# An attention and mixer kernel: 254 steps near its start in another order, other PSUM banks behind them, and 22 unread matmuls split in two

## The chip, the cores and the metric

The kernel runs on one core of a Trainium2 chip. The metric is the device time of one execution in microseconds (us), as the median of several runs. A difference of less than about half a per cent is near what the runs of one kernel differ by among themselves.

## The reference

Inputs are `q`, `k`, `v` of shape 8 x 8 x 576 x 64 (batches, heads, positions, head width) and four weight matrices, all float32. First comes block-causal attention (blocks of 64 positions), then a mixer: one layer pair over the positions (tokens), one over the channels.

```python
scores = (q @ k.T) / 8          # masked to block_i >= block_j, softmax over j
x = softmax(scores) @ v         # -> 8 x 576 x 512 (heads side by side)
xt = x.transpose(0, 2, 1)
h = relu(xt @ w_tok1) @ w_tok2  # 576 -> 256 -> 576
u = x + h.transpose(0, 2, 1)
h2 = relu(u @ w_ch1) @ w_ch2    # 512 -> 1536 -> 512
out = u + h2
```

## The kernel before

The kernel is one long program without loops at run time. Python code lists 1591 small **steps** (a step is a few instructions on one engine), and a written-out string, `ORDER` (L100), says which of them are issued, 1518 in all, in which order and on which engine. A word of it such as `269Tcbda` is step 269, on TensorE (T; A is ScalarE, D VectorE, P GpSimd with the DMAs that it issues, S the DMA queue of SyncE), and the letters behind it are the PSUM banks that the step takes: one bank for each letter, a to d ("mm" in the profile) and e to h ("late"). `placed` (L75) reads the words. Each engine runs its own steps strictly in the order of the words and waits where an operand is not ready.

A bank is taken by a TensorE step, filled, read by VectorE or ScalarE, and given back by the last step that reads it. There are eight banks. When a step takes a bank, its first matmul into it must wait until the last reader of the bank's earlier content has ended, so the letter decides on whom the step waits.

The profile calls the engines PE (TensorE), PEld (its weight loads), DVE (VectorE), ACT (ScalarE), POOL (GpSimd) and SP (SyncE). The steps that matter below, with the line of their instructions:

- Unread matmuls (`raise_clock`, emission at L371 and L378): 11 of 512 columns, then single ones of 256 columns, steps 45 to 154, of which the order issues 37 (45 to 81). They multiply zeros while the first inputs arrive, and nothing reads them.
- Score sets (`score_set`, L568): the scores of four heads in 32-row strips of the array; for batch 1 these are 269, 276, 281 (heads 0 to 3) and 301, 308, 313 (heads 4 to 7), for batch 2 among others 445 and 470. From batch 1 on each takes four banks. Their exponentials run on ACT (L774; L587 in batch 0): 270 to 273 belong to 269, one for each head and bank.
- Transposes of q and k by VectorE (L442): 259, 260, 262 and 263 for batch 1's heads 4 to 7.
- Clears of a tail block of the exponentials (`tail`, L601), on DVE or POOL: 217 and 236 for batch 0's heads 4 to 7.
- Head outputs (`head_out`): exponentials times v on PE (L618; batch 0's in two parts of 3 and 7 matmuls, such as 222 and 223 for head 4, 226 and 227 for head 5, 241/242 and 245/246 for heads 6 and 7), then a reciprocal (L638) and a product (L644) on DVE, which gives the bank back. The last 64 positions go apart (`ends_out`): PE L671 (230 and 249 for batch 0's later heads, 298 and 330 for batch 1), DVE L693 and L699 (193 and 194).
- The token layers: `token_up` (PE L809 and L813, then a relu on ACT L795 or DVE L797; 337, 339, 341, 343 for batch 0, 502 to 505 for batch 1) and `first_uT` or `token_mix` (PE L904).
- The channel layers: `channel_up` for batch 0 (PE L1032), later `channel_up_half` (L1105) and `channel_up_fast` (L1232), `channel_down_fast` (L1366), and transposes of four 128-column matmuls each (`turn`, L1388).

Loads of weights and of later batches go through POOL's DMA queue in the order of the words; outputs go through SP's. POOL's own steps and the DMAs that it issues share one queue.

Of the kernel before, what the change touches and what calls it, by code (L numbers as in the profile page):

```python
# [27 lines left out]
class Plan:  # L28
# [73 lines left out]
    47Tb 48Tb 49Ta 50Ta 37P 51Ta 52Ta 53Ta 54Ta 55Ta 56Ta 35P 57Ta 7D 174Tst 175T 34P 195A 58Ta 59Ta 60Ta  # L102
    61Ta 196A 62Ta 38P 197D 63Ta 31D 64Ta 65Ta 66Ta 176A 199Tt 36P 177A 178D 67Ta 179D 68Ta 33D 69Ta 255P 70Ta 200A
    180Ts 27D 198P 71Ta 72Ta 40P 73Ta 181A 29D 182Tt 157P 74Ta 75Ta 76Ta 183A 77Ta 201Ts 43P 78Ta 79Ta 80Ta 253D
    202A 42P 214Tt 254D 188Tb 189T 41P 215A 184Tc 11D 233Ts 6D 190D 191D 258P 192Td 211Ta 234A 220Tt 216P 256D 39P
    185T 257D 221A 81Tb 218Ts 155P 212D 213D 207Tb 235D 208T 186D 219A 158P 187D 237Tt 193D 209D 156P 203Ta 210D
# [4 lines left out]
    305A 425D 354Td 355T 302A 313Tcbfh 279A 356D 306P 387Tg 353A 267P 426D 384Td 315A 388T 266P 316A 404Ta 385T 317A  # L111
    268P 408Tb 314A 381Te 386D 405A 416Tf 427P 409D 390Tc 389A 307P 391T 333D 430P 372Td 392A 308Tabhg 167P 373T
    311A 334D 382T 168P 310A 369Tc 309A 370T 169P 417A 375Tb 335D 434P 312A 378Ta 379T 383A 433P 366Th 374A 367T
    422D 371A 436P 400Td 423D 376T 380A 289Tc 377A 295Ta 290D 298Tf 368A 291D 330Tb 296D 401A 297D 292Tc 299D 286Tg
    331D 332D 438Tadeh 300D 287D 293D 288D 324Tb 440A 294D 357Tf 325D 439A 321Tc 326D 363Tg 428D 442A 364T 322D 441A
    323D 450Tbdah 431D 365A 318Tc 429D 454A 358T 453A 319D 327Te 432D 360Tg 451A 320D 361T 452A 328D 329D 482Tcabh
    362A 443D 359D 502Te 444P 483A 435P 393D 485A 604P 484A 504Td 503A 437P 170D 486A 470Tcbag 595P 505A 171D 601P
    473A 445Tfehd 471A 172D 514Ta 448A 508Tc 472A 173D 515A 512Th 506Tb 446A 509D 510Ta 474A 513D 397Tcf 447A 475P
    507D 449A 476P 394D 598P 477Tbghe 398A 403Td 395D 480A 479A 511D 481A 493Th 396D 520Ta 478A 490Tg 518Te 521A
    494D 407T 406D 519A 495D 597D 464Ta 596D 455Te 461Th 410D 458Tb 399T 465D 491D 456D 457D 462D 459D 466D 411T  # L120
    463D 600D 402D 496Ta 522Te 412D 516Th 413T 523A 497D 599D 419S 517A 460D 762P 492D 499Te 414D 759P 467Tb
    612Thgcd 498D 526D 415T 336D 615A 616A 614A 530Tca 613A 487Td 500D 468D 469D 531Tg 533A 501D 617P 527D 545Thb
    532A 418D 618P 536T 611P 548A 524Te 488D 489D 534Tg 537A 525D 610P 551T 528D 535A 624Tdecf 605D 608P 552A 538T
    606D 628A 607P 540T 529D 627A 539D 678Th 626A 609P 603D 625A 549Tc 602D 679A 619Tdfge 541D 550A 546Th 622A 760D
    553T 623A 763D 543T 620A 547D 676Tg 621A 761D 544A 644Tdehf 542D 926P 677A 554D 555T 647A 764D 560Tag 648A 556D
    561Tc 929P 563A 680Th 557D 765P 562A 684Tf 681D 645A 566T 558T 685D 646A 564Tc 567A 649D 559D 651Tdhef 650P 565A
    768P 638Ta 653A 635Tb 772P 639D 568T 652A 640D 570T 636D 654A 637D 686Ta 569D 655A 656Tbdhe 571D 641Tc 660A 687D
    629Tf 659A 573T 642D 630D 689S 643D 632Ta 658A 631D 682Te 572D 657A 788Tcfdh 633D 634D 574A 673Tb 683D 790A
    670Ta 674D 789A 664Tg 688S 675D 671D 579Tef 672D 791A 665D 792A 666D 769D 783Tbagc 580A 667Td 784A 661Th 668D
    581T 785A 669D 662D 786A 663D 767D 787A 776Tdhba 582D 842Tc 779A 766D 778A 575D 932P 840Tb 780A 941P 770D 777A  # L130
    583Ta 930D 773P 841A 576D 843A 781P 820Tdgeh 939P 577D 585T 771P 821A 578D 824A 775P 584D 694Tbc 850Td 774P 690D
    697A 587T 586D 822A 935P 691D 823A 782P 692D 698Th 851D 848Tg 588D 699A 700T 849D 695Td 701A 704T 696D 702T 589T
    705D 703D 693D 808Tabde 931D 707T 590D 810A 844Tg 812A 846Th 845D 809A 793Tb 591T 708A 847D 811A 794D 795D 813P
    815Tacde 592D 814P 805Tb 1024P 819A 802Tg 594S 806D 818A 799Th 807D 854S 803D 724Tfe 817A 800D 709Tdb 801D 816A
    727D 710Tc 712A 725Th 927D 711A 728Ta 855S 928D 726A 715T 804D 796Tc 729A 934D 730T 716A 713Th 933D 731A 734T
    420S 797D 798D 714A 732T 593S 735D 943Tcgdf 733D 719T 945A 736D 717T 946A 720D 831Ta 944A 834Tg 718D 737T 947A
    722T 835D 836D 738A 828Td 948P 832D 833D 950Tgchf 723A 829D 830D 837Ta 721D 953A 852Tb 838D 952A 839D 857D 825Td
    951A 853D 876Tea 1036P 954A 877Tc 858D 856S 879A 826D 861Tbh 827D 1035P 878A 862Tg 859D 864D 891Tfd 949P 863A
    880Tc 940P 706D 894A 882T 739D 881A 942P 865Tg 897T 937D 866A 938P 867T 936D 883A 884T 860D 1021P 868A 871T 885D
    1030P 869T 898A 886T 872D 1027P 987Tbcef 870D 874T 887D 1034P 990A 895Tg 988A 875D 889T 991A 1007Te 740D 989A  # L140
    896A 890D 955Tbchf 741D 892Ta 959A 899T 1026D 956A 901T 893D 958A 1009Tf 957A 1008D 902D 975Tbach 1010D 972Te
    978A 904T 900D 979A 960Tf 1025D 969Tc 905A 743Tgh 961D 976A 973D 1122P 974D 962D 977A 970D 971D 982Tefdb 980D
    744A 981D 1022D 966Ta 984A 963Tc 1023D 745T 985A 967D 888D 1119P 986A 964D 965D 983A 1037P 995Td 968D 873A 998Tc
    746D 1050Tabfe 1033P 996D 999D 992Tg 1000D 1054A 749T 993D 1053A 994D 997D 1052A 1028D 1038Tcdge 1051A 1029D
    1004Tb 1041A 1031D 1001Ta 1125P 1040A 747Tf 1032D 1039A 1002D 1003D 1128P 1005D 1006D 1082Tdcga 1135P 748D
    1017Tb 1084A 742D 751T 1083A 1018D 1086A 750D 1042A 1045Tcdba 1085A 752D 1043P 753T 1047A 1131P 1121D 757S 1049A
    1120D 1044P 1048A 1077Tdegf 754D 1064Ta 1080A 1124D 1061Tb 755T 1046A 1065D 1062D 1063D 1079A 1078A 1070Tbcge
    1081A 756D 1067Td 1074A 1123D 1058Tf 1073A 1104Th 1066D 1059D 1071A 1060D 1130D 1072A 1055Ta 1143Tfbeg 1105A
    1056D 1075P 1057D 1015Tc 1134P 1068D 1146A 1127D 1013Ta 1145A 1069D 1102Th 1129D 1147A 1076D 1144A 1014D 1093Td
    1103A 1090Tb 1016D 1136Taegf 1126D 1020S 1099Tc 1137A 1094D 1114Th 1091D 1092D 1140A 1100D 1087Ta 1101D 1139A  # L150
    903D 1096Tb 1088D 1112Tc 1138A 1089D 758S 1108Tf 1095D 1115A 1141P 1113D 1106Ta 1132P 1175Tdgeh 1097D 1142D
    1098D 1011Tc 1133P 1107D 1179A 1336Tb 1177A 1012D 1178A 1109D 1168Tachg 1176A 1110Te 1116S 1171A 910Tdf 1170A
    1111D 1337A 1169A 1334Tc 1117S 911D 906D 1148Tbahe 912T 907D 1150A 1019S 1172A 1151A 916T 1173P 913D 1152A 1174P
    1149A 908D 1118S 1180Tadgh 909D 1153Tb 1183A 914Te 1154D 1184A 1155D 1181A 917D 1194Tb 1182A 1335D 1159Tg 1191Th
    1195D 1185Ta 1196D 1197Td 1160D 1192D 1165Tb 1193D 920T 915D 1161D 1198D 1199D 1166D 1188Th 1167D 921D 1162Td
    1156Tb 1189D 1249Tcg 1190D 918T 1163D 1164D 1252A 1200D 1201D 922T 1186D 919D 1157D 1255T 1158D 924S 1279Ted
    1187D 923D 1280Tb 1282A 1350Ta 1256A 1281A 1234Tch 1351A 1344Tf 1237A 1283Tb 1345D 1285T 1284A 1240T 1286A
    1338Ta 1241A 1250Tf 1339D 1253Te 1251A 1287T 1202D 1254A 1348Tc 1288D 1203D 1259T 1349A 1257T 1238Ta 1258D 1289T
    1239A 1235Tb 1290D 1342Tc 1236A 1244T 1291D 1343D 1356Tf 1242T 1245D 1219Tbc 1243D 1360Te 1260D 1220Ta 1361A
    1357D 1262T 1222A 1292T 1364S 1263D 1221A 1340Te 1247T 1293D 1223Ta 1341D 1358Td 1224A 1246D 1204Tfg 1359D 1248A  # L160
    1205Te 1225T 1207D 1206A 1264Tdh 1226A 1229T 1479D 1267A 1265Te 1230D 1208Tb 1266A 1227T 1480D 1209D 1270T
    1268Te 1271A 1214T 1269D 1212T 1354Td 1215D 1274T 1228D 1232T 1275D 1217T 1272T 1481D 1218A 1210T 1482D 1233A
# [1404 lines left out]
```

## Time and profile before

| | |
|---|---|
| runs, us | 283.47, 284.16, 284.64 (median 284.16) |
| the profiled execution: time | 284.69 us |
| its span, first to last instruction | 282.9 us |
| PE busy | 97% of the span |
| DVE busy | 84% |
| ACT busy | 63% |
| POOL busy | 26% |
| granted TensorE clock, mean | 1.000 |

The span is what the views of the trace cover; some 1.8 us of the execution lie outside it. Times in the views count from the start of the span. The view of the waits lists how long an engine stood still and on whose account. The view of the stretches gives the busy time of each engine between two points in time. The timeline lists instructions with their start, their length, line, shape and number. PE's matmuls overlap one another in these records, so the distance from start to start says more than a length.

### The profile page before, as it was taken

To read this page: it belongs to the slowest core of one execution; us is meant where nothing else is said; L and a number is where in the kernel's file an instruction comes from. 1 tells how busy PE (TensorE), PEld (TensorE's weight loads), DVE (VectorE), ACT (ScalarE), POOL (GpSimd) and SP (SyncE) were. 2 spreads that over 40 slices of the span, in tenths; PEclk is the share of its full clock that TensorE was granted. 3 is DMA by queue.
4 is the path that set the end of the run, shared out by engine and by line. 5 is a ranking of instruction groups with operands and counts; after the bars stand their busy time and mean duration, and the time that the engine had idled before them with its cause. 6 is when DMAs were issued, how large, how long until landed. Compare 5 with 4: busy or idle time off the path is not lost.

```text
span 282.9 us, 9352 instructions
## 1 busy us (share of the span) xinstructions
PE 275.3 (97%) x3982; PEld 204.0 (72%) x3982; DVE 238.9 (84%) x515; ACT 179.2 (63%) x331; POOL 72.7 (26%) x126
## 2 busy tenths in 40 slices
PE   7899999999999999999999999999999999999994
PEld 3466556588776788986877658756789876568884
DVE  3688669999889998999998979859896997579984
ACT  3798788953998856897879866274533744652200
POOL 8895870511631351063232221000000000000000
PEclk9999999999999999999999999999999999999999
DMA  7999999954979492999598594100044502200157
GB/s 163 160 178 192 202 190 206 152 92 86 142 87 139 87 150 56 250 109 170 66 118 139 56 188 60 70 10 19 0 84 95 196 0 76 75 1 2 74 151 224
DMA packets 64890, 31.95 MB, mean 113 GB/s; under 512 B 53200, under 2 KB 55888, under 8 KB 64848
## 3 DMA queue, kind: packets, MB, share of 16 engines
q0 software_dynamic: 44896, 17.49, 53.6%
q1 hardware_dynamic: 19520, 13.21, 18.2%
q8 instruction: 31, 0.51, 0.7%
q10 hardware_dynamic: 432, 0.66, 0.7%
q14 instruction: 11, 0.09, 0.1%
HBM read 35.85 MB, written 9.44 MB: 160 GB/s over the span
## 4 chain that ended last, share of the span: by engine, by line
PE 87%; DMA 4%; ACT 3%; POOL 3%; DVE 1%; issue 1%; POOLq 0%; DVEq 0%
PE late L1366 23%; PE mm L1105 8%; PE mm L1232 7%; PE mm L1366 7%; PE late L1232 6%; PE mm L568 6%; PE late L1105 6%; DMA qk_sb<-in_k_dram 4%; PE mm L618 4%; PE mm L809 3%; PE mm L904 2%; PE late L904 2%; PE late L618 2%; PE mm L1032 2%; ACT e_sb L774 2%; PE late L809 2%
## 5 line engine op out<-in xcount | busy, mean ns | idle before, releaser
L774 ACT ACTIVATE e_sb<-mm 128x512 bf16<-128x512 f32 x82 | 46.6, 606 | 13.1 <-PE late L568 9.4
L774 ACT ACTIVATE e_sb<-late 128x512 bf16<-128x512 f32 x86 | 48.5, 609 | 9.0 <-PE late L568 8.2
L442 DVE STREAM_TRANSPOSE qk_sb<-qk_sb 128x288 int32<-128x288 int32 (+1 forms) x65 | 41.8, 694 | 4.9 <-DMA qk_sb<-in_q_dram 1.8
L468 POOL DMA_DIRECT2D vals<-in_v_dram x45 | 36.9, 832 | 4.5 <-PE mm L618 2.4
L1366 PEld LDWEIGHTS <-gT 128*128 128x128 bf16 x336 | 32.0, 98 | 5.6 <-issue 0.4
L1366 PEld LDWEIGHTS <-sums 128*128 128x128 bf16 x324 | 31.3, 98 | 5.3 <-issue 0.4
L568 PEld LDWEIGHTS <-qk_sb 32*64 32x64 bf16 (+1 forms) x1152 | 19.0, 103 | 14.8 <-issue 11.1
L568 PE MATMUL mm<-qk_sb 32*64 32x64 bf16 (+7 forms) x504 | 26.9, 277 | 0.1
L618 PEld LDWEIGHTS <-e_sb 128*128 128x128 bf16 x640 | 23.1, 97 | 5.3 <-issue 2.2
L568 PE MATMUL late<-qk_sb 32*64 32x64 bf16 (+7 forms) x504 | 26.2, 283 | 0.6 <-issue 0.3
L1366 PE MATMUL late<-wd_sb,gT 128*128 128x256 bf16 x168 | 20.7, 273 | 0.0
L1366 PE MATMUL late<-wd_sb,sums 128*128 128x256 bf16 x168 | 20.6, 273 | 0.0
L1105 PEld LDWEIGHTS <-ws_sb 128*128 128x128 bf16 x192 | 18.2, 98 | 3.1 <-issue 0.9
L618 PE MATMUL mm<-vals,e_sb 128*128 128x65 bf16 x450 | 19.8, 193 | 0.5 <-DMA vals<-in_v_dram 0.3
L644 DVE TENSOR_TENSOR x_sb<-mm,rinv 128x256 bf16<-128x256 f32 x45 | 18.7, 422 | 1.3
L1412 DVE TENSOR_TENSOR o_sb<-late,u_sb 128x512 f32<-128x512 f32 x22 | 15.0, 684 | 3.6 <-PE late L1366 3.6
L1232 PEld LDWEIGHTS <-ws_sb 128*128 128x128 bf16 x120 | 11.7, 98 | 8.6 <-issue 0.2
L1105 PEld LDWEIGHTS <-wc_sb 128*128 128x128 bf16 x144 | 15.3, 114 | 1.5 <-issue 0.4
L1366 PE MATMUL late<-wc_sb,gT 128*128 128x256 bf16 x132 | 16.2, 273 | 0.0
L596 POOL COPY vals<-e_sb 128x256 bf16<-128x256 bf16 (+1 forms) x11 | 4.3, 393 | 39.7 <-ACT e_sb L774 39.6
L400 ACT COPY mm<-late 128x512 f32<-128x512 f32 (+1 forms) x16 | 9.1, 570 | 8.1 <-PE late L1232 5.4
L795 ACT ACTIVATE gT<-mm 128x512 bf16<-128x512 f32 x21 | 12.6, 616 | 1.9 <-PE mm L1105 0.9
(198 smaller groups left out, 630.7 us busy)
## 6 DMA issues: line engine op xcount, KB each, us to landing
out_dram<-o_sb SPq DMA_DIRECT2D x19, 256.0 KB, 3.0
qk_sb<-in_k_dram POOLq DMA_DIRECT2D x14, 288.0 KB, 6.0
qk_sb<-in_q_dram POOLq DMA_DIRECT2D x14, 288.0 KB, 5.9
vals<-in_v_dram POOLq DMA_DIRECT2D x28, 128.0 KB, 4.5
out_dram<-o_sb SPq DMA_DIRECT2D x7, 512.0 KB, 3.8
wc_sb<-in_moe_w_ch_dram POOLq DMA_DIRECT2D x8, 192.0 KB, 7.5
wc_sb<-in_moe_w_ch_dram POOLq DMA_DIRECT2D x3, 512.0 KB, 10.5
vals<-in_v_dram POOLq DMA_DIRECT2D x15, 64.0 KB, 5.3
```

What stands on the lines that cost most here:

```text
L442: nc.vector.transpose(dst[:, 0:S, :] .rearrange("p s e -> p (s e)") .bitcast(I32) .rearrange("p (a k) -> p k a", k=NB)[:, k0:k1], raw2.bit ...
L468: nc.gpsimd.dma_start(out=t[128 - p : 128, J, hs, 0:64], in_=src)
L568: nc.tensor.matmul(out=home(n)[rows, c : c + w], lhsT=bar[r, 0] if j is None else kT[i][r, keys, par], rhs=bar[r, 1] if j is None else qT[ ...
L618: nc.tensor.matmul(out=u[:, I, 0:65], lhsT=e[:, h, c : c + 128], rhs=vt[:, J, head, 0:65], start=(J == 0), stop=(J == I),)
L644: nc.vector.tensor_tensor(out=xt[:, 0:4, 64 * head : 64 * head + 64], in0=u[:, :, 0:64], in1=ri[:, 0:4].to_broadcast([128, 4, 64]), op=MULT,)
L774: nc.scalar.activation(dst, bank_of(x), EXP, scale=scale)
L795: nc.scalar.activation(dst, src, RELU)
L809: nc.tensor.matmul(out=ps, lhsT=w1_sb[:, c, tt : tt + 255 : 2], rhs=xt[:, c, cols], start=(c == 0), stop=False)
L1105: nc.tensor.matmul(out=bank_of(bank)[:, 256 * o_ : 256 * o_ + 256], lhsT=x(o_, m), rhs=y[:, :, m, :], start=opens, stop=m == 1, skip_group ...
L1232: nc.tensor.matmul(out=bank_of(bank)[:, 128 * c : 128 * (c + step)], lhsT=x(m), rhs=y[:, c : c + step, m, :], start=opens, stop=m == 1, sk ...
L1366: nc.tensor.matmul(out=bank_of(bank)[:, 256 * i : 256 * i + 256], lhsT=x[:, kk, 128 * i : 128 * i + 128], rhs=y[:, kk], start=first and i ...
L1412: nc.vector.tensor_tensor(out=dst, in0=src, in1=other, op=ADD)
```

## The change

Two things change.

1. `ORDER`. The words up to step 210 stay. The next 254 words (to just before step 398, in the profile of before about 20 to 57 us) are the same steps in another order. Some steps go to another engine: the clears and copies 217, 236 and 443 from DVE to POOL; 306, 307 and 476 from POOL to DVE; 338, 347, 356, 359, 386 and 409 from DVE to ACT; 340, 353, 362, 380, 401, 417 and 503 from ACT to DVE. Behind step 398 every step stays on its engine and in its place, but the bank letters change: of 225 later steps that take banks, 211 have other letters.
2. The first 22 of the single unread matmuls (steps 45 to 66) are each written as two matmuls of 128 columns instead of one of 256.

The diff, cut to the first words, the last ones of the reordered part, two rows of renamed banks, and the code:

```diff
-    204T 238A 194D 239Ts 261P 205D 206D 164P 8D 240A 236D 269Tcbda 424P 271A 163P 281Tefgh 270A 166P 259D 273A 217D
-    226Tb 283A 227T 284A 222Tc 223T 228D 241Ta 242T 282A 229D 165P 249Tf 224D 245Tg 285A 225D 162P 246T 230Tb 243D
-    244D 339Tc 159P 250D 231D 232D 337Ta 251D 247D 161P 340A 260D 272A 276Tbfeh 338D 348Tc 262D 160P 278A 349T 263D
-    345Ta 280A 346T 248D 277A 341Td 350D 421P 301Tgbfh 274D 347D 264P 343Tc 342D 303A 275D 351Ta 304A 265P 352T 344D
...
+    212D 213D 207Tb 235D 208T 186D 219A 158P 187D 237Tt 193D 209D 156P 203Ta 210D 238A 204T 236P 205D 206D 261P 239Ts 8D
+    194D 164P 240A 269Tbcad 217P 271A 272A 281Tefgh 424P 222Tc 270A 223T 224D 225D 284A 226Ta 227T 245Tb 246T 228D 229D
+    163P 260D 283A 230Tc 166P 249Tg 241Ta 242T 250D 273A 231D 285A 165P 339Tf 282A 345Td 232D 348Tc 337Th 247D 248D 338A
+    340D 251D 259D 276Tgfbe 243D 162P 279A 159P 244D 346T 274D 347A 161P 160P 349T 262D 277A 354Ta 280A 341Th 263D 350D
+    342D 343Td 278A 421P 301Tecgb 351Th 352T 344D 353D 304A 264P 355T 305A 390Td 356A 302A 313Thbgf 314A 303A 275D 387Ta
...
-    1098D 1011Tc 1133P 1107D 1179A 1336Tb 1177A 1012D 1178A 1109D 1168Tachg 1176A 1110Te 1116S 1171A 910Tdf 1170A
...
-    1187D 923D 1280Tb 1282A 1350Ta 1256A 1281A 1234Tch 1351A 1344Tf 1237A 1283Tb 1345D 1285T 1284A 1240T 1286A
...
+    1098D 1011Tf 1133P 1107D 1179A 1336Ta 1177A 1012D 1178A 1109D 1168Tfhde 1176A 1110Tc 1116S
...
+    1187D 923D 1280Ta 1282A 1350Te 1256A 1281A 1234Thf 1351A 1344Ta 1237A 1283Te 1345D 1285T 1284A 1240T 1286A 1338Ta
...
-    WARM, KEEP = 11, 110
+    WARM, KEEP, HALVED = 11, 110, 22
...
-            def emit(o, bank=bank):
-                nc.tensor.matmul(
-                    out=bank_of(bank)[:, 0:256], lhsT=zeros[:, 0:128], rhs=zeros[:, 0:256],
-                    start=True, stop=True,
-                )
+            def emit(o, bank=bank, w=128 if n < HALVED else 256):
+                for c in range(0, 256, w):
+                    nc.tensor.matmul(
+                        out=bank_of(bank)[:, c : c + w], lhsT=zeros[:, 0:128], rhs=zeros[:, c : c + w],
+                        start=c == 0, stop=True, skip_group_check=c > 0,
+                    )
```

More of the change, by code (lines that the diff above doesn't have):

```diff
@@ L111 @@
[L111 to L120, printed above, removed]
@@ L179 @@
+    1578Ta 1546S 1543D 1560T 1572D 1544T 1573D 1581D 1553D 1558Tf 1561D 1545D 1564T 1579D 1548S 1549A 1559D 1584T 1565D
+    1582T 1577D 1585D 1566T 1589A 1583D 1556T 1588A 1567D 1562T 1569S 1557D 1586T 1563D 1568S 1587D 1590S
 """
```

127 lines of the change are left out of this document (66 added, 61 removed).

## The prediction

> **What bounds the kernel now.** I read the page first, then the stretches, then the waits of PE, and then the timeline wherever a wait lay.
>
> ```profile
> PE 275.3 (97%) x3982; PEld 204.0 (72%) x3982; DVE 238.9 (84%) x515; ACT 179.2 (63%) x331; POOL 72.7 (26%) x126
> ...
> PE 87%; DMA 4%; ACT 3%; POOL 3%; DVE 1%; issue 1%; POOLq 0%; DVEq 0%
> ```
>
> PE is busy for 97% of the span, and the chain of work that ended last runs through PE for 87% of it. So what counts is the time in which PE stands still: a wait that is taken away there brings the end forward, a wait that is added puts it off.
>
> ```profile
> 56.00:63.00 7.00, 7.00 (x140) 6.24 (x138) 6.93 (x15) 4.68 (x10) 1.19 (x3) 1.00 0.65 111
> 63.00:70.00 7.00, 7.00 (x149) 6.21 (x147) 6.64 (x19) 2.02 (x4) 1.06 (x2) 1.00 0.35 64
> 112.00:180.00 68.00, 68.00 (x1304) 52.31 (x1301) 63.65 (x155) 52.43 (x102) 17.54 (x28) 1.00 0.87 125
> ```
>
> In the stretches the second number is PE (full, at granted clock 1.00) and the fourth is DVE: 6.93 and 6.64 of 7 us, 63.65 of 68. So behind the reordered part nothing is to be won on PE, and DVE, which hands most banks back, is nearly full beside it. Where DVE still idles, it waits for PE; so the two keep their distance, and a wait of PE is not made good later.
>
> ```profile
> PE late L568 <- issue: 0.3, 1, 0.3
> PE late L568 <- ACT e_sb L587: 0.3, 1, 0.3
> PE mm L618 <- DMA vals<-in_v_dram: 0.3, 1, 0.3
> PE mm L618 <- DVE e_sb L601: 0.2, 1, 0.2
> ```
>
> These four of the six waits of PE are all that the view shows between 20 and 57 us. The reordering can win little more than them.
>
> **The reordered part, gains.** First the clear.
>
> ```profile
> 21.98 0.72 DVE L442 STREAM_TRANSPOSE qk_sb<-qk_sb 128x288 int32<-128x288 int32 x1 [1.39 <-DMA qk_sb<-in_k_dram]
> 22.76 0.11 DVE L601 MEMSET e_sb<- 64x64 uint32 x1
> ```
>
> ```profile
> 22.28 0.45 PE L618 MATMUL mm<-vals,e_sb 128*128 128x65 bf16 x9 [0.28 <-DMA vals<-in_v_dram]
> 22.93 0.36 PE L618 MATMUL mm<-vals,e_sb 128*128 128x65 bf16 x6 [0.21 <-DVE e_sb L601]
> ```
>
> The clear 217 is queued on DVE behind transpose 259, which waits for its DMA. Nine matmuls start in 0.45 less the last one's own 0.19 us, so every 0.03 us; the tenth was due at 22.57 and started at 22.93. In the new order POOL does 217, ahead of the load 424, and no transpose stands before it: 0.36 gained. On POOL, 236 delays the loads 261 and 164, and 217 then 424; two memsets, an estimated 0.6 us at most from the 0.11 us on DVE and a slower engine. I count nothing, because the transposes of 261 and 424 come later in the new order; without that cover it would be 0.6. The wait for the v load (0.28) stays: its place in POOL's order does not change. So does the wait for ACT (0.3): ACT's order up to step 240 is the same.
>
> ```profile
> 23.67 0.32 PE L671 MATMUL late<-vals,e_sb 128*64 128x65 bf16 x8
> 23.82 0.20 PE L671 MATMUL late<-vals 128*64 128x65 bf16 x2
> 23.95 0.24 PE L618 MATMUL late<-vals,e_sb 128*128 128x65 bf16 x2
> ```
>
> Second, neighbours. The ten matmuls of 249 hold PE for 0.28 us, of which their starts fill at most 0.19 (0.15 to the ninth, and the same step on); about 0.09 is the change of tile shape. The new order puts 230 and 249 side by side (two changes fewer) and 298, 330 and 438 (one fewer): 3 x 0.09 = 0.27 gained.
>
> ```profile
> 52.00 0.64 ACT L795 ACTIVATE aT<-mm 128x512 bf16<-128x512 f32 x1
> ```
>
> ```profile
> 52.23 0.39 PE L568 MATMUL late<-qk_sb 32*64 32x448 bf16 x2
> 52.70 0.36 PE L568 MATMUL mm<-qk_sb 32*64 32x448 bf16 x1
> ```
>
> Third, score set 445. Its fourth bank comes from relu 505, which ends at 52.64; PE goes on at 52.70. That is the price of handing a bank over: 0.05 us behind the reader's end. PE loses 52.70 - 52.23 = 0.47. In the new order 503 leaves ACT, so 505 starts earlier; between nothing and 0.47, and I take 0.15, since 505 still has to follow PE's 504.
>
> ```profile
> 28.50 0.28 PE L568 MATMUL late<-qk_sb 32*64 32x256 bf16 x1
> 29.10 0.27 PE L568 MATMUL late<-qk_sb 32*64 32x256 bf16 x1 [0.32 <-issue]
> ```
>
> Fourth, score set 301 stops half-way for 29.10 - 28.50 = 0.6 us, of which some 0.55 is lost, and no semaphore releases it ("issue"). I do not know its cause. The change adds 22 matmuls with their weight loads ahead of it and changes the order before it, so it may go or come back: 0 to 0.55 gained, and I take the middle, 0.28.
>
> **The reordered part, losses.**
>
> ```profile
> 20.18 0.55 PE L568 MATMUL mm<-qk_sb 32*64 32x320 bf16 x4
> 20.44 0.22 PE L568 MATMUL mm<-bar 32*64 32x64 bf16 x4
> ```
>
> Score set 269 begins at 20.18 and stops until 20.44, when DVE's product 206 has given its fourth bank back. In the new order the fourth bank (d) comes from 194, which is moved behind 206 on DVE, so about 0.3 us later. PE itself is covered, since 281 waits for ACT's last exponential of batch 0 anyway, but the exponentials of 269 start some 0.2 later, and the head outputs take the banks that those free. Going through the new words with these lengths I find about nine waits of 0.05 to 0.15 us for banks (at 245, 230, 241, 276, 330, 438, 327 and 450 above all), together 0.65, where perfect timing would make it nothing and all nine at 0.15 would make it 1.35.
>
> Sum of the part: 0.36 + 0.27 + 0.15 + 0.28 - 0.65 = 0.41 gained; 0.13 if the stop without releaser stays, 0.68 if it goes. The other exchanges between ACT and DVE (six one way, seven the other) change each engine's load by about one evacuation, and loads that move by a few places have us of slack; I cost them at nothing.
>
> **The unread matmuls.**
>
> ```profile
> 8.30 0.51 PE L568 MATMUL sc<-qk_sb 32*64 32x192 bf16 x28 [1.53 <-DVE qk_sb L442]
> ```
>
> ```profile
> 33.46 0.39 PE L1388 MATMUL mm<-ident,uT 128*128 128x128 bf16 x4
> 33.68 0.59 PE L1032 MATMUL mm<-uT,wc_sb 128*128 128x512 bf16 x2
> ```
>
> Four 128-column matmuls, each with its own weights, take 33.68 - 33.46 = 0.22 us, 0.055 each, so two are as long as one of 256 columns should be, and the split costs nothing. Thirteen of the 22 also lie ahead of PE's wait of 1.53 us before 8.30, which hides them whatever they cost; if the other nine were not free, ACT's exponentials would move with them. The Trainium skill says otherwise (TensorE: Matmul & The Clock Gate, Back-to-back issue gap): a stream of weight loads and 128-column matmuls is sustained at about 81 ns each. By that page the split would add an estimated 0.05 us a pair, and the sum would grow by up to 0.5 us for those nine; the row above disagrees, and I go by the row.
>
> **Behind the reordered part: the banks.** Here the engines' orders are the same, so I set each later bank of the new letters against the trace of before: when does PE reach the step, and when does the bank's new previous reader end?
>
> ```profile
> 57.97 1.09 ACT L774 ACTIVATE e_sb<-late 128x512 bf16<-128x512 f32 x2
> ...
> 59.06 0.19 PE L618 MATMUL late<-vals,e_sb 128*128 128x65 bf16 x1
> ...
> 123.26 0.42 DVE L644 TENSOR_TENSOR x_sb<-mm,rinv 128x256 bf16<-128x256 f32 x1
> ...
> 123.46 0.27 PE L1105 MATMUL late<-th_sb,ws_sb 128*128 128x256 bf16 x1
> ...
> 163.64 0.42 DVE L644 TENSOR_TENSOR x_sb<-mm,rinv 128x256 bf16<-128x256 f32 x1
> 163.71 0.39 PE L904 MATMUL mm<-aT,w_sb 128*128 128x512 bf16 x1
> ...
> 181.93 0.42 DVE L644 TENSOR_TENSOR x_sb<-mm,rinv 128x256 bf16<-128x256 f32 x1
> 182.11 0.38 PE L1232 MATMUL mm<-uT,wc_sb 128*128 128x512 bf16 x1
> ```
>
> Take the pair at 163.7. The L904 matmul is step 1011; before, it took bank c, free for long. Now it takes f, which head output 1096 held and product 1098 gives back. That product ends at 163.64 + 0.42 = 164.06, so with 0.05 for the handover PE would wait until 164.11, for 0.40 us. In the same way 1279 (bank g, from 1158) waits 182.35 + 0.05 - 182.11 = 0.29, 862 (bank h, from 827) 0.27, and the first such take, 493 at 59.06, 0.05. There are 31 such takes of 225, from 493 to 1418 at 228; in before's own choice of letters there is none, since it takes mostly the bank that was freed first, and the new letters often the one freed last.
>
> What do they add up to? All 31: 3.15 us. But takes close together share a wait, as a PE that has waited once is late for the next bank as well. They lie in 11 groups more than 5 us apart, and the largest of each group add up to 1.63. Between groups DVE waits for PE again, so groups add. I take 2.0, nearer the lower end, because most of the shares come from DVE's products, whose queue is backed up within a group.
>
> **The sum.** The profiled execution took 284.69 us, its span is 282.9, and 1.8 lie around it, which the change does not touch. It gives 284.69 + 2.0 - 0.41 = 286.3. That execution is 0.53 above the median of the runs, 284.16; from the median the same difference, +1.6, gives **285.8 us**. The case's own range is from +1.63 - 0.68 to +3.15 - 0.13, so 285.1 to 287.2.
>
> **The rivals.** *The banks come in time (not slower).* The times of release are read from before. If DVE and ACT run earlier against PE behind step 398, every release comes earlier, and from 0.4 us on even 1011's wait is gone. For it: the new order moves the clear 443 and the evacuations 359, 386 and 409 off DVE before 50 us. Against it: 503 and 476 come onto DVE just ahead of step 398, DVE is at 6.93 of 7 us there, and by 70 us it waits for PE again, which restores before's distance. It would leave the part's gain alone: 284.16 - 0.41 = 283.8 us, the same within what can be measured.
>
> *Every stop in the part goes (faster).* The clear, both stops inside score sets and the wait at 20.18 vanish, 0.36 + 0.47 + 0.55 + 0.26 + 0.27 = 1.9, with no new bank waits there and none behind: 282.3 us. Against it: 194 moves the wrong way, and the letters are what they are.
>
> *The stop without releaser multiplies.* If it hangs on the place of an instruction in PE's stream, the added ones shift it into other score sets; twice more costs 1.1, so 286.9 us. PE's waits of before show it once in the whole span, which speaks against it.
>
> **How the numbers follow.** The banks wait as computed: 0.70. They come in time: 0.20. Every stop goes: 0.07. The stop multiplies: 0.03. Half a per cent, about what a measurement of this kernel can tell from no change, is 1.42 us. The first case, from +0.95 to +3.0 about +1.6, exceeds that in about two thirds of its chance, 0.46; with the last case slower is 0.49. Same gets the rest of the first case and nearly all of the second: 0.43. Faster: 0.08. The range reaches from 283.4 (the second case with the whole 0.68) to 287.2. The first case's own range is the 285.1 to 287.2 above.
>
> **What would show it.** PE's waits in the new profile should list waits on DVE's L644 products and ACT's L774 exponentials behind 60 us: at L904 near 164, at L1232 near 182, at L1105 near 123, of about 0.4, 0.3 and 0.3 us. PE should reach step 398's neighbours (L1366 at 55.75 now) 0.1 to 0.7 us earlier, and the wait for the clear L601 should be missing. The prediction is wrong if PE's first L1366 is later than now, or if PE stays without waits from 60 to 250 us.

## The result, and the profile after

The changed kernel takes 287.84 us (median of 6 runs), the kernel before beside it 284.4; the ratio is 1.0113, with a 95% interval of 1.0067 to 1.0159. In 12 further runs it is 287.1 beside 284.5, ratio 1.0084 (1.0054 to 1.0115). So the change is slower, as predicted, but by more than the 1.6 us forecast, and outside the range. In some executions, of the kernel before too, the granted clock falls to a half for 10 to 14 us from about 16 us on, which adds some 3 us; the medians below, and the profiles compared between 15 and 30 us, leave these executions out, and by that the changed kernel has 287.16 us (17 runs), the kernel before 284.44 (126 runs from all comparisons): **+2.7 us**.

The profiled execution took 287.85 us, its span is 286.1 (before 284.69 and 282.9). Its page, busy time of the engines and the chain:

```profile
PE 275.9 (96%) x3983; PEld 206.1 (72%) x4004; DVE 240.7 (84%) x516; ACT 179.4 (63%) x330; POOL 72.3 (25%) x126
...
PE 71%; DVE 6%; issue 1%; ACT 1%; DVEq 0%; DMA 0%
```

These busy times do not tell where the 3.2 us went by which the span grew. The page counts 3983 matmuls beside 4004 weight loads: records of 21 matmuls are missing from this profile. A second profile of the same kernel has them all:

```profile
PE 278.2 (97%) x4004; PEld 206.4 (72%) x4004; DVE 240.0 (84%) x516; ACT 179.4 (63%) x330; POOL 72.2 (25%) x126
```

Of its span of 285.8 us PE is idle for 7.6, as much as before (282.9 less 275.3). The records of matmuls overlap, so a short wait hardly shows in the sum. PE's waits (line of PE, what it waits for, us in total, times, longest); line numbers here are two less than before's, and one or none less in the experiments:

```profile
PE mm L368 <- DVE wd_sb L341: 1.2, 1, 1.2
PE mm L616 <- DMA vals<-in_v_dram: 1.2, 3, 0.8
PE sc L566 <- DVE qk_sb L440: 1.0, 1, 1.0
PE late L902 <- DVE x_sb L642: 0.2, 1, 0.2
PE mm L669 <- DVE x_sb L642: 0.2, 1, 0.2
PE mm L566 <- DVE x_sb L642: 0.2, 1, 0.2
PE mm L855 <- issue: 0.2, 1, 0.2
```

The wait for the clear (L601 before) and the stop in score set 301 are gone. The wait for ACT's L587 is gone from the list only: score set 281 starts 1.2 us behind 269 in both kernels, and 269 now spends more of that time waiting for its fourth bank. The waits for v's loads have grown from 0.3 to 1.2 us, and three waits for DVE's products (now L642) are new. The last row is no stop: two of the missing records leave a gap there, and the second profile has none. The stretches that the prediction read, after:

```profile
56.00:63.00 7.00, 6.90 (x123) 5.92 (x122) 6.85 (x14) 5.12 (x10) 1.14 (x3) 1.00 0.61 101
63.00:70.00 7.00, 7.00 (x162) 6.26 (x159) 6.88 (x21) 1.30 (x3) 1.05 (x2) 1.00 0.27 84
112.00:180.00 68.00, 67.41 (x1314) 52.08 (x1305) 62.67 (x151) 52.79 (x102) 18.18 (x30) 1.00 0.90 125
```

PE had 68.00 of 68 us from 112 to 180; now it has 67.41, and 67.76 in the second profile, which has all records. Each loss is small, so totals hide them; what shows them is the start of the same step in both traces, found by following the words of ORDER. Against before, PE starts step 184 (15.5 us) 0.17 us later, 339 0.51, 397 (the first L1366) 0.37, 403 0.53, 520 (59.4) 0.79, 862 (123.5) 1.48, 1011 (163.7) 1.98, 1279 (182.1) 2.43, and from there on 2.43 or 2.44 to its last step. The last store then lands 0.63 us later behind its issue. In the timeline (start, length, instruction, in brackets the idle time before it):

```profile
23.02 1.08 PE L616 MATMUL mm<-vals,e_sb 128*128 128x65 bf16 x30 [0.83 <-DMA vals<-in_v_dram]
24.31 0.32 PE L669 MATMUL mm<-vals,e_sb 128*64 128x65 bf16 x8 [0.20 <-DVE x_sb L642]
...
46.88 0.42 DVE L642 TENSOR_TENSOR x_sb<-mm,rinv 128x256 bf16<-128x256 f32 x1
47.36 0.38 PE L566 MATMUL mm<-qk_sb 32*128 32x512 bf16 x1 [0.17 <-DVE x_sb L642]
...
165.21 0.42 DVE L642 TENSOR_TENSOR x_sb<-late,rinv 128x256 bf16<-128x256 f32 x1
165.69 0.38 PE L902 MATMUL late<-aT,w_sb 128*128 128x512 bf16 x1 [0.22 <-DVE x_sb L642]
```

The last pair is the prediction's step 1011: the product that holds bank f ends at 165.63, PE goes on at 165.69, and step 1011's delay grows from 1.70 to 1.98 us. Predicted were 0.40 of it, and the handover of 0.05 us is there.

### The profile page after: what moved, and what is told of

It reads as the page before. It is cut to its first block, busy times and chain, and to the rows that moved or that the text cites. A ratio compares the mean times of both kernels' runs of the same rounds, so it can differ in the third digit from the quotient of the medians.

```text
span 286.1 us, 9349 instructions
## 1 busy us (share of the span) xinstructions
PE 275.9 (96%) x3983; PEld 206.1 (72%) x4004; DVE 240.7 (84%) x516; ACT 179.4 (63%) x330; POOL 72.3 (25%) x126
## 4 chain that ended last, share of the span: by engine, by line
PE 71%; DVE 6%; issue 1%; ACT 1%; DVEq 0%; DMA 0%
PE late L1364 15%; PE mm L1364 12%; PE late L1103 7%; PE late L1230 7%; PE mm L1103 6%; PE mm L1230 6%; PE mm L566 3%; PE late L566 3%; PE mm L616 2%; PE mm L807 2%; PE late L616 2%; PE late L902 2%; PE late L807 1%; DVE x_sb L642 1%; DVE u_sb L917 1%
## 5 line engine op out<-in xcount | busy, mean ns | idle before, releaser
L772 ACT ACTIVATE e_sb<-mm 128x512 bf16<-128x512 f32 x85 | 48.6, 605 | 7.7 <-PE mm L566 4.5
L566 PE MATMUL late<-qk_sb 32*128 32x512 bf16 (+7 forms) x478 | 26.6, 282 | 0.0
L616 PE MATMUL mm<-vals,e_sb 128*128 128x65 bf16 x380 | 16.9, 193 | 1.2 <-DMA vals<-in_v_dram 1.2
L642 DVE TENSOR_TENSOR x_sb<-mm,rinv 128x256 bf16<-128x256 f32 x38 | 15.9, 422 | 1.1
L398 ACT COPY mm<-late 128x512 f32<-128x512 f32 x18 | 10.5, 583 | 9.8 <-PE late L1230 5.8
L1103 PEld LDWEIGHTS <-wc_sb 128*128 128x128 bf16 x144 | 15.3, 114 | 1.4 <-issue 0.4
L1364 PE MATMUL late<-wd_sb,sums 128*128 128x256 bf16 x114 | 14.1, 273 | 0.0
L416 POOL DMA_DIRECT2D qk_sb<-in_q_dram x14 | 7.7, 547 | 25.4 <-DVE x_sb L642 10.7
L1230 PEld LDWEIGHTS <-wc_sb 128*128 128x128 bf16 x90 | 10.0, 113 | 5.3 <-issue 0.4
L793 ACT ACTIVATE gT<-mm 128x512 bf16<-128x512 f32 x19 | 11.2, 606 | 4.0 <-PE mm L1230 2.4
L793 ACT ACTIVATE gT<-late 128x512 bf16<-128x512 f32 x19 | 11.4, 610 | 3.3 <-PE late L1103 2.6
## 6 DMA issues: line engine op xcount, KB each, us to landing
wc_sb<-in_moe_w_ch_dram POOLq DMA_DIRECT2D x3, 512.0 KB, 10.3
```

The lines of the kernel that those rows point to most:

```text
L398: nc.scalar.copy(dst, src)
L566: nc.tensor.matmul(out=home(n)[rows, c : c + w], lhsT=bar[r, 0] if j is None else kT[i][r, keys, par], rhs=bar[r, 1] if j is None else qT[ ...
L616: nc.tensor.matmul(out=u[:, I, 0:65], lhsT=e[:, h, c : c + 128], rhs=vt[:, J, head, 0:65], start=(J == 0), stop=(J == I),)
L642: nc.vector.tensor_tensor(out=xt[:, 0:4, 64 * head : 64 * head + 64], in0=u[:, :, 0:64], in1=ri[:, 0:4].to_broadcast([128, 4, 64]), op=MULT,)
L772: nc.scalar.activation(dst, bank_of(x), EXP, scale=scale)
L793: nc.scalar.activation(dst, src, RELU)
```

## The experiments

Medians in us, beside the kernel before in the same comparison (for several series together, beside all its runs). The differences are uncertain by some 0.4 to 1 us to either side: resampling the runs gives 95% intervals of 1.2 to 2.7 for the new letters alone, 0.4 to 1.1 for the three halved series together (+0.8), -0.1 to 0.7 for the part alone. So below the traces say where PE loses time, and the medians whether that is about all.

| kernel | us (runs) | before | difference |
|---|---|---|---|
| changed, both series | 287.16 (17) | 284.44 | +2.7 |
| old letters behind step 403 | 285.34 (11) | 284.42 | +0.9 |
| new letters behind alone | 286.19 (9) | 284.42 | +1.8 |
| halved alone, three series | 285.12, 285.15, 285.55 (8, 10, 11) | 284.42, 284.30, 284.55 | +0.7, +0.85, +1.0 |
| changed, not halved, two series | 286.91 (10) | 284.44 | +2.5 |
| 22 quartered alone | 285.28 (11) | 284.51 | +0.8 |
| part alone | 284.82 (12) | 284.51 | +0.3 |
| part, first-freed letters | 284.76 (11) | 284.51 | +0.25 |
| last-freed letters behind alone | 298.18 (4) | 284.30 | +13.9 |
| first 13 halved | 284.38 (8) | 284.30 | +0.1 |
| last 9 halved | 284.11 (8) | 284.30 | -0.2 |
| 22 more matmuls, two series | 284.79 (20) | 284.44 | +0.35 |
| 22 at half the columns | 284.14 (11) | 284.28 | -0.1 |
| part, 503 and 476 back | 284.64 (8) | 284.42 | +0.2 |

**The changed kernel again.** No edit.

> The changed kernel once more, unedited, for a second profile of it. In the first one the span grew by 3.2 us: 0.4 by the time PE reaches step 397 (first L1364 product), 2.06 more up to 185 us, and 0.7 behind PE's last matmul, where the last store took 2.70 us to land and before only 2.07. Theory A (the bank letters behind step 403 cost 2.0 us, the rest is loads and stores that landed late in that one execution): the 2.06 between the first L1364 product and 185 us comes again within 0.2, while the waits for the v loads near 15 and 23 us and the last store's landing differ from the first profile by some tenths. Theory B (the part's new order of loads causes the late v loads): the v load of step 39 lands again at about 23.0 us, against 22.2 before. Time by A and B: 286.6 to 288.0.

Between steps 403 and 1279 its PE loses 1.81 us (0.26 to 2.07; 1.90 in the first profile), in the same places. The v load of step 39 lands at 22.42 us, not 23.0, so theory B falls: the late v loads differ from execution to execution. But the last store takes 2.71 us again. That is no chance, and theory A was wrong to put it down to one execution.

**Which letters behind step 403.** Two kernels: the changed one with the old letters there, and the kernel before with the new ones. Both sets are renamed to fit the eight banks that are held at step 403; 199 words differ, for instance

```diff
 changed kernel, old letters behind:
-493Tb 862Th 1011Tf 1279Tcg
+493Tg 862Tb 1011Td 1279Taf
 kernel before, new letters behind:
-493Th 862Tg 1011Tc 1279Ted
+493Tg 862Tf 1011Td 1279Tbh
```

> The changed kernel up to step 403; behind it each bank take gets the bank that the same step had given back in the kernel before (the old letters, renamed so that they fit the eight banks as they stand at step 403). Theory A (bank letters): the 2.06 us that the changed kernel lost between the first L1364 product and 185 us are gone, so PE's start of step 1234 stands at most 0.6 us behind that of the kernel before; time 285.5 to 286.0, about 2 us less than the changed kernel. Rival C (DVE and ACT leave the part in a worse state, and the loss behind it is theirs, whatever the letters): still some 2 us between these places, time about 287.8.

> The kernel before up to step 403; behind it the new letters (renamed so that they fit). The part and the unread matmuls are as before. Theory A: PE loses 1.6 to 2.4 us between the first L1364 product and 185 us, at L1105 near 123, L904 near 164 and L1232 near 182 among others; time 286.0 to 286.8. Rival C: nothing is lost there, time 284.4 within 0.4.

Theory A holds, rival C falls: the old letters take 1.8 us from the changed kernel (to 285.34, a little under the range given), the new ones add 1.8 to the kernel before. With the old letters PE loses nothing behind step 520 but one stop of 0.59 near 92 us; with the new ones alone it loses 1.60 between 403 and 1279. The five profiles with the new letters lose the same at the same steps (0.28 or 0.29 at 1011, 0.26 or 0.27 at 1279, 0.15 or 0.16 at 862), and none with the old letters loses anything there. Step 1011 in that kernel, with the old order up to 403:

```profile
167.78 0.42 DVE L643 TENSOR_TENSOR x_sb<-mm,rinv 128x256 bf16<-128x256 f32 x1
...
168.26 0.59 PE L903 MATMUL mm<-aT,w_sb 128*128 128x512 bf16 x2 [0.22 <-DVE x_sb L643]
```

It is the same wait of 0.22 us, on the same product.

**The bank freed last.** The kernel before; behind 403 each take gets the bank that was freed last.

```diff
-493Th 531Tg 678Th 676Tg
+493Te 531Th 678Th 676Te
```

> The kernel before up to step 403, whole unread matmuls; behind it each take gets, of the banks that are free and of the same kind at that place, the one that was given back last. The prediction's method (a take waits until its bank's previous reader ends in the trace of before, plus 0.05 us, less the delay that the reader itself has by then) gives 2.08 us for the new letters of the change, where 1.6 to 2.06 were measured, and for these letters 16.3 us in about 58 waits (without sharing among them 24.0, more than is thinkable). Theory A: 284.5 + 16.3 = 300.8, and 297 to 303 allowing for its error. Rival C' (the banks were only a part of it: once PE is late, DVE and ACT catch up and give banks back earlier, so that waits stop adding up): 288 to 294, with PE's waits dying out behind the first 60 us.

298.2 lies in the range of theory A (297 to 303), near its lower end. Waits go on adding up: PE is 4.2 us behind the kernel before at step 583 (97 us), 11.3 at 1279 and 13.3 from 1483 (206 us) on. So C' falls; the method asks some 17% too much (16.3 for 13.9). PE's waits in it, some of a long list:

```profile
PE late L617 <- ACT e_sb L773: 1.3, 4, 0.4
...
PE mm L567 <- DVE gT L796: 0.6, 1, 0.6
PE late L808 <- DVE half L401: 0.6, 1, 0.6
PE late L1365 <- ACT e_sb L773: 0.5, 2, 0.3
PE late L808 <- ACT e_sb L773: 0.5, 2, 0.3
PE late L808 <- DVE gT L1143: 0.4, 1, 0.4
```

PE waits here for ACT's exponentials and for evacuations by DVE, for which it did not stand still behind step 403 before: same work, same order, other banks.

**The part alone.** New order up to 403, old letters behind, unread matmuls whole; and the same with the letters of the part chosen anew (258 words differ).

> The new order up to step 403 alone: old letters behind it and whole unread matmuls. With both it had 285.3 against 284.4. The prediction had a gain of 0.41 for this part: 284.0. By what was measured (285.3 with halving, less 0.7): 284.6. If the halving costs nothing under the new order: 285.3.

> As the part alone, but the letters between steps 269 and 403 are chosen anew: each take gets the bank that was given back first, by the releases in the trace of the kernel with old letters behind. Theory A (letters that are given back late cost in the part too, about 1 us in waits at 230, 346, 352, 450, 482, 445 and 512): 0.5 to 1.0 below the part alone, so 283.7 to 284.1 if that is at 284.6. Rival (waits in the part come from loads and from ACT's exponentials, whatever the letters): the same as the part alone within 0.3.

The part costs about 0.3 instead of gaining 0.41. First-freed letters remove the wait at 450 (0.18 us idle) and one of 0.17 at score set 477, and PE needs 0.47 us less from step 184 to 403; but about 0.25 of that is a stop without releaser just ahead of score set 301, which the profile of the part alone has by itself, and at step 520 it gives 0.17 back. What is left is too little for these medians, so the two theories stay undecided on the time.

At two places the kernels with the new part lose time, and by the same amounts in every profile. The first is score set 477. Its second bank comes from DVE's sum 507 (L919); first before, then the part alone:

```profile
55.86 0.68 DVE L919 TENSOR_TENSOR u_sb<-mm,x_sb 128x512 bf16<-128x512 f32 x1
...
57.15 0.38 PE L568 MATMUL mm<-qk_sb 32*64 32x448 bf16 x1
```

```profile
56.40 0.69 DVE L919 TENSOR_TENSOR u_sb<-mm,x_sb 128x512 bf16<-128x512 f32 x1
56.98 0.53 PE L568 MATMUL mm<-qk_sb 32*64 32x448 bf16 x2
...
57.15 0.38 PE L568 MATMUL mm<-qk_sb 32*64 32x448 bf16 x1
```

Before, the sum ends at 56.54, 0.6 us ahead of PE. With the new part it ends at 57.09; PE begins the set at 56.98 and goes on with its other banks from 57.15. From 477 to 403 PE needs 0.75 us instead of 0.58 in six profiles of seven (0.58 with first-freed letters, which give the set other banks).

The second is step 520: PE's delay against before grows by 0.26 us there in six profiles of seven (by 0.43 with first-freed letters). Transposes 520 (L991) read DVE's sum 511 (L919); first before, then the part alone:

```profile
58.34 0.68 DVE L919 TENSOR_TENSOR u_sb<-mm,x_sb 128x512 bf16<-128x512 f32 x1
...
59.36 0.39 PE L991 MATMUL mm<-ident,u_sb 128*128 128x128 bf16 x4
```

```profile
58.87 0.68 DVE L919 TENSOR_TENSOR u_sb<-late,x_sb 128x512 bf16<-128x512 f32 x1
...
59.61 0.40 PE L991 MATMUL late<-ident,u_sb 128*128 128x128 bf16 x4
```

Before, the sum is done 0.33 us before PE comes (59.03 and 59.36). With the new part it is done at 59.55, and PE starts 0.06 behind it. Next, two steps are put back:

```diff
-503D ... 476D
+503A ... 476P
```

> The part alone (new order up to step 403, old letters behind, whole unread matmuls) with two steps put back on the engines that they had before: the product 503 on ACT, the clear 476 on POOL. In every kernel with the new part PE loses 0.26 us at step 520, whose transposes wait for DVE's sum 511; before, 511 ends 0.33 us ahead of it. Between 51 and 57 us DVE does 503 (0.6 us of its time) and 476 (0.28) in the new part and not in the old one. If these two make DVE late, 511 is done at least 0.1 us before PE reaches step 520, nothing is lost there, and the profile is some 0.26 us shorter behind it; the time may then be 284.3 to 284.8, which hardly differs from 284.8. If DVE is late for another reason, or ACT's 503 now makes step 445 wait (0.2 to 0.5, as before the change), no gain behind step 403.

```profile
58.30 0.68 DVE L919 TENSOR_TENSOR u_sb<-late,x_sb 128x512 bf16<-128x512 f32 x1
...
59.34 0.39 PE L991 MATMUL late<-ident,u_sb 128*128 128x128 bf16 x4
```

Now 511 ends at 58.98, 0.36 ahead, nothing is lost at 520, and from 477 to 403 PE needs 0.58 us again: these two steps (0.68 and 0.16 us of DVE's time) made DVE late. But score set 445 stops half-way for 0.5 us again, as before the change. That is less of a gain than it looks, because with 503 on DVE the set starts later: its first bank waits for 503, which ends at 52.19 there and at 51.65 on ACT. From 470, the set before it, to 514, the step behind it, PE needs 1.41 us in the part alone, 1.51 before and 1.54 with the two steps back. So moving them to DVE gains 0.1 at 445 and loses 0.17 at 477 and 0.26 at 520, five and seven microseconds on. The net 0.3 is about what the part costs: PE's last step stands 0.25 us behind the kernel before in the part alone and 0.01 ahead of it with the two steps back. The medians (284.82 and 284.64) are too close to show it by themselves.

**The unread matmuls.** First the halving alone.

```diff
-    WARM, KEEP = 11, 110
+    WARM, KEEP, HALVED = 11, 110, 22
...
+            def emit(o, bank=bank, w=128 if n < HALVED else 256):
+                for c in range(0, 256, w):
...
```

> The kernel before, its order and letters, with the 22 unread matmuls halved and nothing else. The reasoning of the prediction: no difference, 284.4 within 0.4, since PE waits before its first score set anyway. Rival D (the 22 extra matmuls with their weight loads make the instruction stream of PE longer, its instruction fetch comes earlier, 12.7 instead of 13.2 us, and pushes back the v loads that PE waits for at 15 and 22 us): 0.4 to 0.8 us slower, with waits for vals of about 1 us in the profile instead of 0.3.

> The kernel before with the 22 unread matmuls halved, once more: it had 285.1 against 284.4, while taking the halving out of the changed kernel gave nothing. If the 0.7 is real it comes again, 0.5 to 0.9; if it was chance, within 0.3. Its profile should show where: PE's start of step 184 (15.5 us before), or a stop without releaser.

It comes again: +0.7 and +0.85. But it is not in the opening (in the second profile PE starts step 184 0.14 us earlier than before), and not a price for each matmul:

> The kernel before, with the first 22 unread matmuls cut into four of 64 columns: 66 more matmuls, where the halving has 22 more. Theory D1 (each added matmul costs, so the price grows with their number): three times 0.7, so about 286.5. Theory D2 (what costs is only that PE's fetches of instructions fall on another moment of the v loads): no such growth, anything between 284.0 and 285.3, with the fetch before 15 us earlier than the 12.7 of the halved kernel. Rival (nothing): 284.4.

> The kernel before with only the first 13 of the 22 halved, those that stand before the first score set, where PE waits anyway. By the prediction nothing: 284.4. If PE's longer instruction stream costs through fetches, whatever covers it: 0.4 or more. If the cost is PE's time between the first score sets: nothing here and all of it in the run with the other nine.

> The kernel before with only the last nine of the 22 halved, those between the score sets of batch 0. Prediction: nothing. If the cost of halving is PE's time there (0.05 to 0.1 us for each of the nine): 0.4 to 0.9.

Sixty-six more matmuls cost the same 0.8 as 22 more; 13 or 9 more show no cost, within about 0.6. D1 falls. What the second profile of the halving shows is two stops without releaser, which end at 28.1 and 93.1 us. The second one in the timeline, and the instruction fetches in 90.5 to 91.8 us (packets, MB, share):

```profile
92.20 0.33 PE L618 MATMUL mm<-vals,e_sb 128*128 128x65 bf16 x5
93.11 0.33 PE L618 MATMUL mm<-vals,e_sb 128*128 128x65 bf16 x5 [0.59 <-issue]
```

```profile
q8 instruction: 1, 0.02, 4.6%
```

That one packet is 16 KB of instructions and starts at 90.71 us in the trace; PE goes on 2.40 us behind its start. The stop of the prediction, in score set 301 before, ends at 29.10, 2.44 us behind the start of such a packet at 26.66. Two further edits are to separate count from width (both shown against the halved kernel):

```diff
 22 at half the columns:
-            def emit(o, bank=bank, w=128 if n < HALVED else 256):
-                for c in range(0, 256, w):
+            def emit(o, bank=bank, w=128 if n < HALVED else 256, end=128 if n < HALVED else 256):
+                for c in range(0, end, w):
 22 more under cover:
-            def emit(o, bank=bank, w=128 if n < HALVED else 256):
-                for c in range(0, 256, w):
+            def emit(o, bank=bank, cut=(0, 96, 192, 256) if n < 11 else (0, 256)):
+                for c, e in zip(cut, cut[1:]):
```

> The kernel before with the first 22 unread matmuls at 128 columns and no second half: no instruction more than before, half the columns. Halving into two costs 0.7 us (285.1, 285.3, 285.2 in three runs), 13 or 9 of them alone nothing. Theory F (the cost comes with the number of instructions, which moves the places where PE runs out of fetched instructions: with 44 more it stops 0.6 to 0.8 us inside the head output of step 667 near 92 us): nothing here, 284.1 to 284.7, no stop at 667. Rival G (the cost comes with the short columns, by PE's activity or the time of the first score sets): 0.5 to 0.9 here too.

> The kernel before with the first 11 unread matmuls cut into three (96, 96 and 64 columns): as many instructions more as by the halving of 22, the same columns, all of them ahead of PE's wait before the first score set. Theory F: about 0.7 again, 284.9 to 285.4, with a stop without releaser of 0.4 to 0.8 us about 2.4 us behind the start of a fetch of 16 KB, near 92 us. Rival G (short columns between the score sets): nothing, 284.1 to 284.7.

> The kernel before with the first 22 unread matmuls at 128 columns and no second half: 3982 matmuls as before, 22 of them with half the columns. (The run called 22 at half width read the loop's last value and ran the halved kernel once more: 4004 weight loads in its profile.) Theory F (the price comes with PE's instruction count, which moves its fetches): nothing, 284.1 to 284.8, and the last fetch of 16 KB stands as in the kernel before, 7.5 us ahead of the last store's landing, with that store landing in about 2.1 us. Rival G (short columns): 285.0 to 285.5.

> The run with 22 more under cover, once more, because its 0.3 (interval -0.2 to 0.9) tells nothing apart. Theory F: 0.5 to 0.9. Rival G: within 0.3. Its last 16 KB fetch stood 12.4 us ahead of the end, as in all kernels with 22 more.

As the third text says, the first of these four ran the halved kernel a third time (+1.0). The proper one costs nothing: so not the short columns, and G falls. Twenty-two more matmuls with the old columns cost +0.3 and +0.5 (together 0.35, from 0 to 0.7), in direction as F has it, half its size, and without a stop near 92 us in its two profiles. The halved kernel has that stop in two of its three profiles (0.76 and 0.45 us of PE's time), the changed kernel in neither of its two. The kernel with 13 halved has a stop of 0.62 us near 28 us in its profile and no cost in its median. So the width is out as a cause and the count remains; that the stops carry the price is not shown, and the cause of the price stays open.

**The changed kernel without halving.**

> The changed kernel, order and letters as they are, with the 22 unread matmuls whole again (256 columns each). Halving alone has cost the kernel before 0.7 us (285.1 against 284.4, in executions whose granted clock stays above 0.99). Theory D (halving costs 0.7 us wherever it stands, through the loads of v that PE waits for at 15 and 22 us): 286.4 to 286.7, against 287.1 to 287.4 with halving. Rival (the 0.7 was chance, or the new order hides it): 287.1 to 287.4.

> The changed kernel with whole unread matmuls, once more: it had 287.5 in only five undisturbed executions, against 287.2 with halving in 17. If halving costs 0.7 here too: 286.4 to 286.7. If the changed kernel's stops fall elsewhere and halving is free in it: 287.0 to 287.5. In the changed kernel the last store took 2.70 and 2.71 us to land; without halving 2.25 in one profile, and it should be so again.

287.48 (5 runs) and 286.81 (5), together 286.91: halving costs the changed kernel some 0.25 us, but the interval is -0.5 to 1.0, which tells it apart neither from nothing nor from the 0.8 of the old kernel. What the profiles do show is the last store. The row of the last 128 KB store (issues, KB, us from issue to landing), changed kernel, the same not halved, and the kernel before:

```profile
out_dram<-o_sb SPq DMA_DIRECT2D x1, 128.0 KB, 2.7
```

```profile
out_dram<-o_sb SPq DMA_DIRECT2D x1, 128.0 KB, 2.3
```

```profile
out_dram<-o_sb SPq DMA_DIRECT2D x1, 128.0 KB, 2.1
```

## Why the prediction was wrong

The forecast was +1.6 us, and +2.7 was measured. The step that failed is the reordered part: a gain of 0.41 was forecast and a loss of about 0.3 came (-0.1 to 0.7), 0.7 of the 1.1 us that are missing. Most of that loss is a term that was put at nothing, the exchange of steps between ACT and DVE. A second term put at nothing, the halved matmuls, measured 0.25 in this order (not clear of nothing) and 0.8 in the old one, with its cause open. The largest term, the letters, held.

**The letters behind the part: right in kind and nearly in size.** Predicted 2.0, measured 1.8 in time by both swaps, and 1.55 to 1.64 between steps 520 and 1279 in four profiles of the changed kernel, with halving and without. Steps 1011, 1279 and 862, predicted at 0.40, 0.29 and 0.27, add 0.28, 0.26 and 0.15. All 31 summed would have been 3.15; the largest of each group alone, 1.63, is what PE loses, so that takes close together share a wait fits. The 2.0 in between was a choice, and behind 1279 nothing more is lost, though takes up to 228 us were counted. The rule used for the bank freed last, which lets the reader's end move with the delay that it has gathered, asks too much both times: 2.08 for 1.6 here, 16.3 for 13.9 there.

**The reordered part: wrong sign.** Predicted -0.41, measured +0.3 in time. By its steps:

- The clear, and 230 next to 249: predicted 0.54 gained between 281 and 339. The clear's wait is gone, but this stretch goes by when v's loads land: PE needs 2.97 to 3.59 us with the new part (median 3.05 of seven profiles) and 3.12 to 3.50 with the old order (median 3.16 of eight). About 0.1 was gained, and even that is inside the spread. In the changed kernel's own profile 230 waits 0.20 us for DVE instead.
- Score set 445: predicted 0.15 of 0.47; from 470 to 514 PE needs 1.40 or 1.41 us instead of 1.51 or 1.52, so 0.11. This term was right.
- The stop in score set 301 was taken at half. It is no property of the order: the old order shows such a stop near 28 us in some of its profiles, not in others, and PE's time from 339 to 397 is 31.11 with it and 30.56 in the profile with the new letters alone, which has none. So a stop in one profiled execution was counted as if it belonged to the kernel. Without such a stop, six profiles of the old order need 30.55 to 30.79 us there and four of the new part 30.96 to 30.98: the new part loses 0.2 to 0.4 in this stretch. Beside the profile of before this does not show, as its own stop costs 0.55 there.
- Bank waits, 0.65: those at 230 and 450 are there, 0.20 and 0.17 us idle in the changed kernel's timeline.
- Not in the sum at all: 0.17 at score set 477 and 0.26 at step 520, both because 503 and 476 make DVE late. The prediction named this, "503 and 476 come onto DVE just ahead of step 398", and used it against a rival; in the sum, it cost the exchanges between ACT and DVE at nothing. Behind step 398 it checked bank takes alone and not the data that PE waits for from DVE. Here the two steps put back show the cause.

By the prediction's own sign the first L1366 should have come 0.1 to 0.7 us earlier. It came 0.37 and 0.09 us later in the changed kernel and 0.22 earlier in one of its profiles without halving: it carries the opening's spread, and one profile could not have decided by it.

**The halved matmuls: the reason held, the term did not.** "The split costs nothing" compared PE's time for 128 and 256 columns, and that is so. The nine of them between the score sets, first before, then in the changed kernel:

```profile
8.96 1.16 PE L378 MATMUL mm<-wd_sb 128*128 128x256 bf16 x9
```

```profile
8.72 1.18 PE L376 MATMUL mm<-wd_sb 128*128 128x128 bf16 x18
```

Eighteen halves take 0.02 us more than nine whole ones, 0.056 us from start to start. The rule of the Trainium skill that was set against it (TensorE: Matmul & The Clock Gate, Back-to-back issue gap) gave about 81 ns each and by the prediction's estimate up to 0.5 us; the trace disagrees, and that this sum lies near the 0.25 to 0.8 measured is chance. What failed is the assumption that an instruction costs only its own time; what it costs besides stays open.

Together: part +0.3, letters +1.6 to 1.8, halving +0.25 in this order, 2.15 to 2.35 of the 2.7 measured. The rest is within the uncertainty of these medians, and 0.2 of it may be the last store, which lands later in the changed kernel even without halving (2.25 and 2.30 us against 2.07). The rivals are out: no bank came in time by itself (PE's delay still grows at 182 us, and up to 206 us with the bank freed last), and not every stop went. The stop without releaser did not multiply in the changed kernel: its two profiles show one such stop behind 20 us, of 0.13 us.

## What to carry to other kernels

Where a written-out order picks buffers by name, the choice of the buffer is a wait of its own: with the same work and order, the new choice cost 1.8 us and the bank freed last 13.9 against the old choice, which mostly takes the bank freed first. When a step moves to another engine, walk that engine's queue forward until it idles, and check everything that waits on it there, data as well as buffers: here 0.84 us more for DVE cost PE 0.43 five and seven microseconds later. And a stop that no semaphore explains, seen in one execution, is not yet a term of a sum: ask a second profile of the same kernel.

## What the hardware showed that was not expected

**Stops of PE behind a packet of instructions.** Ten times behind 20 us, in nine of the twenty profiles, PE stands idle for 0.09 to 0.72 us before an instruction that waits for no semaphore (gaps left by missing records not counted). Each of these stops ends 2.25 to 2.50 us behind the start of a 16 KB instruction packet, whatever PE does there (score sets, token layers, head outputs, channel layers). Most such packets bring no stop. If PE waits there for its instructions, the places where its stream is cut into packets matter, and 44 unread instructions near 6 us can move a stop to 92 us. That the packet makes the stop is read from these coincidences; no run moved a packet and nothing else.

**The last store's landing.** With 22 more matmuls the last 16 KB packet starts 12 to 13 us before the last store lands, without them 7.3 to 7.7 us, and the last store takes 2.14 to 2.42 us instead of 1.93 to 2.07 under the old letters or order. But three kernels break the pattern: 1.76 us with 13 halved (packet 10.2 us ahead), 2.13 with nine halved (10.3), 2.03 with the 22 quartered (17.2). Under new part and new letters together an 8 KB instruction packet starts 3.4 to 3.5 us before the landing: 2.25 and 2.30 us without halving, 2.70 and 2.71 with it. Whether the packets delay the store is not shown, and the 16 KB one, which takes 0.9 to 1.6 us, is over more than 4 us before the store is issued.
